# Fourteen small copies moved from VectorE to GpSimd in a scheduled attention kernel, together with a newly searched plan

## Chip, cores and metric

One core of a Trainium2 chip. The metric is the device time of one execution in microseconds (us). An execution's time is about 1.8 us more than the span of its profile, so the two are not mixed below. Every run also reports its span and the mean clock granted to TensorE (1.000 is full speed). All runs told here count as fast.

## The reference

Two attentions on the same x (2048 x 640, bf16), mixed by a gate. Cut:

```python
g = _sigmoid((x * gate_w).sum(-1, keepdims=True))
a = _A_ref(x, A_wqkv, A_wo)   # full softmax attention, 32 heads of 20, 2048 x 2048 scores per head
b = _B_ref(x, B_wqkv, B_wo)   # each token looks at 8 positions, itself first, 2 apart: s, s-2, ..., s-14
return g * a + (1 - g) * b
```

Branch A has 32 x 2048 x 2048 exponentials. They set the time. Branch B is small and is fitted in beside them, 256 tokens at a time.

## The kernel before

The kernel does not write its instruction order down. A list scheduler inside it, run when the program is built, gives each operation an assumed duration and decides what comes next on each engine. The numbers in `PLAN` are its thresholds, changed every few score tiles; they come from an offline search.

```python
PLAN = {
    0: ((0.34, 0.64), 0.37, 6.3, 2.5, 0.51, -1.0, -0.1, 11.8, 4.5, 7.2, 0.52, 0.47, 4.4, 1.86, 0.0, 0.85, 2, 0.0),
    ...                                   # 49 entries in all
}
...
# at score tile s:
plan = PLAN.get(s) if acting else None
if plan:
    (SLACK, XTOL, XPRIO, XLATE, DWAIT, DIDLE, DIDLE2, DTIME, DLOW, DLATE, DVE_AHEAD, DAHEAD, BOOST, XBOOST, RFILL,
     FILL, HOLD, BOFF) = plan
```

The loop over score tiles: TensorE makes 2 or 3 blocks of 128 x 512 scores (`qk`), ScalarE takes their exponentials in one instruction (`exp`), TensorE multiplies the results with V two tiles later (`pv`). Some blocks "ride" along to VectorE, which makes their exponentials by integer arithmetic (`uD`, then shifted copies `eD`). Between tiles the scheduler spends TensorE's free time on projections and on branch B, and where its load is under `FILL`, on filler matmuls with a zero or throw-away result:

```python
def exp(s):
    n = len(tiles[s])
    exps[s] = T("act", actc(512 * n), lambda e: e.activation(
        ebuf[s % NE][:, 0:512 * n], score[s % 2][:, 0:512 * n], ACTF.Exp, scale=LN2 / STEP), ...)

def filler(limit):
    if sch.load(2.3) >= FILL:
        return False
    ...   # four matmuls of 512 columns, each on a quarter of the columns of the array
```

The part touched: each step of branch B needs the last 16 K and V columns of the step before it, and copies them to the front of its tile before the new columns are written.

```python
def TB(dur, *a, **k):          # VectorE work of branch B; bdone paces it against BALL
    bdone[0] += dur
    return T("dve", dur, *a, **k)

if u > 0 and m > 0 and f0 == 0:
    bb, key = ((kB, "kB"), (vB, "vB"))[m - 1]
    TB(0.15, lambda e, bb=bb: e.tensor_copy(bb[:, :, 0:PADB], bb[:, :, TOK:TOK + PADB]),
       reads=[key], writes=[key], port=True)
```

## Time and profile before

| | kernel before |
|---|---|
| time | 836.07 us (835.97 to 836.23, 3 runs) |
| ScalarE busy | 803.9 of 835.4 us |
| ScalarE waiting for scores, after the first exponential | 7.6 us |
| head / middle / tail | 19.6 / 804.2 / 11.6 us |

The head ends at the start of the first exponential, the middle at the end of the last. To read such a kernel, ask of each of the three what sets it: a fixed chain in the head, ScalarE's work and gaps in the middle, TensorE's queue in the tail. The prediction shows the lines.

### The profile page before, as it was taken

What the parts mean: (1) busy time and instruction counts of PE and PEld (TensorE: products, weight loads), DVE (VectorE), ACT (ScalarE), POOL (GpSimd) and SP (SyncE); (2) the same over time, 40 slices, a digit from 0 to 9 for tenths busy, and PEclk for the clock granted to TensorE, in tenths of its full rate; (3) what the DMA queues carried; (4) which work ended last, traced back from release to release, by engine and by line L of the source; (5) the groups of instructions that cost most, each with busy time, mean ns of one, the idle gap of its engine ahead of it and who ended that gap; (6) DMA issues with size and microseconds to landing.
All of it is one profiled execution on the core that took longest, in us unless ns stands there. A gap on an engine that the chain in (4) does not pass through costs nothing.

```text
span 835.4 us, 29602 instructions
## 1 busy us (share of the span) xinstructions
PE 789.3 (94%) x12599; PEld 289.9 (35%) x12601; DVE 683.7 (82%) x1205; ACT 803.9 (96%) x767; POOL 138.7 (17%) x180
## 2 busy tenths in 40 slices
PE   8999999999999899989998999999999999998997
PEld 4333323334333332333233333333333333333223
DVE  7567888889888887978797988798898898887873
ACT  4999999999999999999999999999999999999994
POOL 5013013431111111011111011111102111101110
PEclk9999999999999999999999999999999999999999
DMA  9112112200111110011001011110011001101100
GB/s 313 30 37 44 33 25 45 73 13 19 29 37 29 29 30 20 7 42 32 20 18 41 18 20 29 36 42 9 5 39 30 10 20 25 38 6 31 32 6 34
DMA packets 45016, 29.15 MB, mean 35 GB/s; under 512 B 27204, under 2 KB 43684, under 8 KB 44884
## 3 DMA queue, kind: packets, MB, share of 16 engines
q1 hardware_dynamic: 44596, 26.92, 12.4%
q8 instruction: 100, 1.64, 0.8%
q10 hardware_dynamic: 288, 0.33, 0.1%
q14 instruction: 32, 0.26, 0.1%
HBM read 11.94 MB, written 2.62 MB: 17 GB/s over the span
## 4 chain that ended last, share of the span: by engine, by line
PE 54%; ACT 30%; issue 10%; DVE 5%; DVEq 0%; ACTq 0%
ACT ebuf L1538 30%; PE score L1515 17%; PE obank L1583 13%; PE side L557 13%; PE score L557 5%; PE obank L1604 2%; DVE uD L1528 1%; PE side L1604 1%; DVE eD L797 1%; PE obank L459 1%; PE score L1230 1%; PE side L885 1%; DVE stage L869 0%; PE score L1604 0%; DVE stage L970 0%
## 5 line engine op out<-in xcount | busy, mean ns | idle before, releaser
L1538 ACT ACTIVATE ebuf<-score 128x1024 bf16<-128x1024 f32 (+1 forms) x735 | 792.6, 1237 | 11.6 <-PE score L1515 9.7
L1515 PE MATMUL score<-qT,kT 32*128 32x512 bf16 x2048 | 291.9, 384 | 31.6 <-ACT ebuf L1538 20.6
L1528 DVE TENSOR_SCALAR uD<-score 128x512 int16<-128x512 f32 x324 | 217.2, 683 | 38.4 <-PE score L1515 36.1
L797 DVE TENSOR_SCALAR eD<-uD 128x2048 int16<-128x2048 int16 x243 | 168.1, 722 | 7.9 <-PE obank L1583 7.2
L1515 PEld LDWEIGHTS score<-qT,kT 32*128 32x128 bf16 x2048 | 75.1, 91 | 282.7 <-ACT ebuf L1538 137.6
L1583 PE MATMUL obank<-ebuf,vA 128*21 128x512 bf16 x1724 | 161.3, 385 | 2.2 <-ACT ebuf L1538 1.8
L789 POOL TENSOR_TENSOR vS<-vA,vw 128x252 bf16<-128x252 bf16 x81 | 61.0, 757 | 291.5 <-PE obank L1583 256.3
L557 PE MATMUL side<-xT,kvw 128*32 128x256 bf16 (+1 forms) x2530 | 103.0, 281 | 3.1 <-DVE qkvB L853 1.4
L1583 PE MATMUL obank<-eD,vS 128*21 128x512 bf16 x972 | 84.1, 382 | 0.0
L557 PEld LDWEIGHTS side<-xT,kvw 128*32 128x32 bf16 x2530 | 59.3, 96 | 37.9 <-issue 22.0
L764 POOL TENSOR_TENSOR rcp<-rcp,gA 128x16 f32<-128x16 f32 x31 | 11.3, 365 | 351.9 <-DVE rcp L762 351.9
L1583 PEld LDWEIGHTS obank<-ebuf,vA 128*21 128x21 bf16 x1724 | 38.6, 89 | 82.3 <-issue 69.5
L970 DVE TENSOR_TENSOR stage<-qkvB,repB 128x1280 bf16<-128x1280 bf16 x64 | 52.9, 856 | 0.7 <-DMA repB<-eB 0.7
L869 DVE TENSOR_TENSOR stage<-qkvB 128x1280 bf16<-128x1280 bf16 x64 | 51.4, 830 | 0.1
L853 DVE CAST qkvB<-side 128x512 bf16<-128x512 f32 (+1 forms) x72 | 41.9, 591 | 10.5 <-PE side L557 10.5
L557 PE MATMUL side<-stage,ident 128*32 128x512 bf16 (+1 forms) x736 | 47.4, 345 | 1.2 <-DVE uD L744 0.5
L1604 PE MATMUL obank<-xT,zero 128*32 128x512 bf16 x444 | 37.9, 385 | 0.0
L770 POOL TENSOR_TENSOR oN<-oTt,rcp 128x512 bf16<-128x512 f32 x31 | 33.0, 1065 | 2.4
L1583 PE MATMUL obank<-uD,vA 128*21 128x512 bf16 x324 | 31.7, 382 | 0.0
L758 DVE STREAM_TRANSPOSE oTt<-obank 128x512 f32<-128x512 f32 x32 | 22.7, 709 | 9.0 <-PE obank L1583 8.9
L1583 PEld LDWEIGHTS obank<-eD,vS 128*21 128x21 bf16 x972 | 24.0, 92 | 17.4 <-issue 4.1
L557 PE MATMUL side<-woA_d,oTd 128*32 128x128 bf16 (+1 forms) x580 | 28.8, 293 | 0.0
(173 smaller groups left out, 555.5 us busy)
## 6 DMA issues: line engine op xcount, KB each, us to landing
repB<-eB SPq DMA_DIRECT2D x128, 32.0 KB
WqP<-in_A_wqkv_dram SPq DMA_DIRECT2D x16, 160.0 KB
stage<-in_B_wqkv_dram SPq DMA_DIRECT2D x1, 2400.0 KB
oTd<-oN SPq DMA_DIRECT2D x108, 20.0 KB
qT<-dst SPq DMA_DIRECT2D x104, 20.0 KB
out_dram<-outsb SPq DMA_DIRECT2D x12, 160.0 KB
kvw<-in_A_wqkv_dram SPq DMA_DIRECT2D x2, 800.0 KB
oTd<-in_A_x_dram SPq DMA_DIRECT2D x2, 640.0 KB
```

The source lines that it names most:

```text
L557: ins = e.matmul(o[j:k, :], l(j) if callable(l) else l[:, j:k], r, start=(first and i == 0), stop=(last and i == n - 1), skip_group_check= ...
L770: T(en, c2, lambda e: e.tensor_tensor(oo, ii, ib, ALU.mult), reads=["rcp", "oTt"], writes=["oN0"])
L789: T("pool", 0.7, lambda e: e.tensor_tensor(vS[:, d % 2, :, :], _ap(vA, (kb * NQ + q) * 4 * DV, [[0, K - 1], [1, 4 * DV]]), _ap(vw, 0, [[1, ...
L797: T("dve", 0.11 + 0.1334 * n, lambda e, k=k, sl=sl: e.tensor_scalar(eD[:, sl % NS, 0:512 * n].bitcast(I16), uD[d % 2][:, 0:512 * n].bitcas ...
L853: t = TB(dvc(n * TOK), lambda e, o=o, i=i: e.tensor_copy(o, i), reads=[("side", b)], writes=[key])
L869: TB(dvc(CN * TOK, 2), lambda e, w=w, ks=ks: e.tensor_tensor(prodB(w), qB[:, :, :], ks, ALU.mult), reads=["qB", "kB"], writes=[("prod", w) ...
L970: TB(dvc(CN * TOK, 2), lambda e, w=w, vs=vs, rr=rr: e.tensor_tensor(prodB(w), vs, rr, ALU.mult), reads=["vB", ("repB", w4 % NR)], writes=[ ...
L1515: ins = e.matmul(o, kT[32 * j:32 * j + 32, q, kb * P:(kb + 1) * P], qT[g % NQT][32 * j:32 * j + 32, :], start=True, stop=True)
L1528: t = T("dve", 0.69, lambda e: e.tensor_scalar(uD[d % 2][:, 512 * i:512 * (i + 1)].bitcast(I16), side[x], UOFF, 0.0, op0=ALU.add, op1=ALU. ...
L1538: exps[s] = T("act", actc(512 * n), lambda e: e.activation(ebuf[s % NE][:, 0:512 * n], score[s % 2][:, 0:512 * n], ACTF.Exp, scale=LN2 / S ...
L1583: ins = e.matmul(obank[32 * j:32 * j + DV, :], v, src, start=(kb == 0), stop=(last and k >= len(lst) - 4), skip_group_check=True)
L1604: ins = e.matmul(o[32 * j:32 * j + 32, :], w[:, 32 * j:32 * j + 32] if best else w[:, :], xT[:, 0, 0:512], start=bool(best), stop=bool(bes ...
```

## The change

Intent: take the 14 copies off VectorE, which carries part of the exponentials, put them on GpSimd, which is mostly idle, and search the plan again for that program. The diff, with the plan cut:

```diff
 PLAN = {
-    0: ((0.34, 0.64), 0.37, 6.3, 2.5, 0.51, -1.0, -0.1, 11.8, 4.5, 7.2, 0.52, 0.47, 4.4, 1.86, 0.0, 0.85, 2, 0.0),
-    ...                                             (49 entries)
+    0: ((0.3, 0.64), 0.31, 2.5, 2.5, 0.49, -1.34, -0.1, 11.8, 7.0, 8.15, 0.52, 0.47, 4.4, 4.0, 0.0, 0.71, 2, 0.0),
+    ...                                             (58 entries)
 }
-                TB(0.15, lambda e, bb=bb: e.tensor_copy(bb[:, :, 0:PADB], bb[:, :, TOK:TOK + PADB]), reads=[key], writes=[key], port=True)
+                T("pool", 0.3, lambda e, bb=bb: e.tensor_copy(bb[:, :, 0:PADB], bb[:, :, TOK:TOK + PADB]), reads=[key], writes=[key])
-    BALL = 172.0
+    BALL = 170.0
```

## The prediction

> **What bounds the kernel now.** I began with the page's busy times and its costliest groups.
>
> ```profile
> PE 789.3 (94%) x12599; PEld 289.9 (35%) x12601; DVE 683.7 (82%) x1205; ACT 803.9 (96%) x767; POOL 138.7 (17%) x180
> ...
> L1538 ACT ACTIVATE ebuf<-score 128x1024 bf16<-128x1024 f32 (+1 forms) x735 | 792.6, 1237 | 11.6 <-PE score L1515 9.7
> L1528 DVE TENSOR_SCALAR uD<-score 128x512 int16<-128x512 f32 x324 | 217.2, 683 | 38.4 <-PE score L1515 36.1
> L797 DVE TENSOR_SCALAR eD<-uD 128x2048 int16<-128x2048 int16 x243 | 168.1, 722 | 7.9 <-PE obank L1583 7.2
> ```
>
> ScalarE (ACT) is busy 96% of the span, almost wholly with the exponentials of attention A (L1538). VectorE takes a share of them: 324 blocks of 512 columns (L1528), each later used through shifted copies (L797). The 11.6 us ahead of the L1538 group is everything ScalarE lost there, 9.7 of it waiting for scores. To place it I cut the execution at the first exponential's start and the last one's end; the columns are the stretch, its length, busy time and instruction count of each engine, then TensorE clock and DMA.
>
> ```profile
> 0.00:19.60 19.60, 16.51 (x129) 9.41 (x135) 14.44 (x34) 8.11 (x10) 12.25 (x21) 1.00 0.95 307
> 19.60:823.80 804.20, 765.29 (x12302) 277.04 (x12302) 664.39 (x1162) 794.65 (x755) 126.45 (x159) 1.00 0.11 28
> 823.80:835.40 11.60, 7.48 (x172) 3.47 (x172) 4.90 (x9) 1.10 (x3) 0.00 (x0) 0.98 0.16 59
> ```
>
> So there are a head of 19.6 us, 804.2 us in which ScalarE (fourth engine) is busy 794.65, and a tail of 11.6 us. 2.1 of the 9.7 us waited for scores is the wait before the very first exponential and belongs to the head; **only 7.6 us of ScalarE waiting is left for a better order to win.** ScalarE's own timeline, read for the rows with an idle time in brackets, shows where:
>
> ```profile
> 22.04 3.28 ACT L1538 ACTIVATE ebuf<-score 128x1024 bf16<-128x1024 f32 x3 [0.97 <-PE score L1515]
> 25.64 29.82 ACT L1538 ACTIVATE ebuf<-score 128x1024 bf16<-128x1024 f32 x30 [0.33 <-PE score L1515]
> 56.38 2.37 ACT L1538 ACTIVATE ebuf<-score 128x1536 bf16<-128x1536 f32 x2 [0.92 <-PE score L1515]
> 305.77 61.65 ACT L1538 ACTIVATE ebuf<-score 128x1024 bf16<-128x1024 f32 x59 [0.41 <-PE score L1515]
> 452.67 5.12 ACT L1538 ACTIVATE ebuf<-score 128x1024 bf16<-128x1024 f32 x5 [0.46 <-PE score L1515]
> 458.42 1.45 ACT L1538 ACTIVATE ebuf<-score 128x1536 bf16<-128x1536 f32 x1 [0.64 <-PE score L1515]
> 460.25 11.34 ACT L1538 ACTIVATE ebuf<-score 128x1536 bf16<-128x1536 f32 x9 [0.37 <-PE score L1515]
> ```
>
> They are a few short waits, in groups. The group at 452 to 460 us coincides with the only stretch where the TensorE clock fell (third figure from the end):
>
> ```profile
> 454.60:458.00 3.40, 2.73 (x25) 0.73 0.18 47
> 458.00:461.40 3.40, 3.33 (x57) 0.77 0.04 7
> ```
>
> Last, the tail, from the timeline:
>
> ```profile
> 823.22 0.60 ACT L1538 ACTIVATE ebuf<-score 128x512 bf16<-128x512 f32 x1 [0.18 <-PE score L1515]
> 823.87 0.40 PE L1583 MATMUL obank<-ebuf,vA 128*21 128x512 bf16 x4 [0.30 <-ACT ebuf L1538]
> 826.42 0.45 DVE L772 STREAM_TRANSPOSE oN<-oN 128x256 f32<-128x256 f32 x1
> 830.07 1.27 PE L1063 MATMUL score<-outsb,oN 128*32 128x128 bf16 x32
> ```
>
> The last product with V starts at 823.87; its normalized result is there at 826.87, but the closing projection (L1063) starts only at 830.07, behind 80 projection matmuls of 512 columns that fill TensorE from 825.31. The tail is TensorE's queue, not the chain through VectorE.
>
> **What the Trainium skill says.** "Perfetto Trace Analysis", Identifying the Most-Contended Engine, takes occupancy as the measure for Vector, Scalar and GpSimd and warns that matmul busy time is not one for TensorE. The trace agrees: TensorE shows 94% while ScalarE gets gapless stretches of dozens of exponentials. "TensorE: Matmul & The Clock Gate", Part 1, says that an idle window of about 3.4 us throttles the array's clock; here 0.73 and 0.77 are granted in the two stretches above, after gaps of 0.4 to 0.5 us around 450 to 456 us, and 1.00 in nearly all the rest. "SBUF — State Buffer", Who interferes with whom, says that GpSimd and a VectorE copy in a two-port mode, or one with two SBUF inputs, exclude each other for a whole instruction. GpSimd's L789 takes 610 ns in the median and 1191 at most, which fits, though no row names the cause. "GPSIMD Engine Reference", Engine selection, calls GpSimd about line rate on one-input work; this case has no small one-input copy there yet.
>
> **Part 1, the copies.** The history copies are these (shown before the bar: 14 instructions, 173 ns each):
>
> ```profile
> L840 DVE COPY qkvB<-qkvB 128x80 bf16<-128x80 bf16 x14 | 2.4, 173 | 0.1
> ```
>
> VectorE loses 14 x 0.173 = 2.4 us of 683.7. GpSimd gains 14 copies; from its rcp product (16 columns, 222 ns median) and vS product (252 columns, 610 ns) I estimate 222 + 64 x 388/236 = 0.33 us each, 4.6 us in all on an engine 17% busy. VectorE has 804.2 - 664.4 = 140 us idle in the middle and hands nothing saved straight to ScalarE: in the built program both kernels give VectorE 324 blocks and 243 shifted copies. Direct worth: 0 to 0.3 us; I write 0.
>
> **Part 2, the plan.** The plan only sets thresholds of the scheduler that runs at build time, so I compared the two built instruction orders. Engines do the same work but for these counts:
> - Exponentials: 479 of 1024, 255 of 1536 and one of 512 columns become 469, 262 and none: 735 to 731 instructions, 1724 blocks in both. In gapless stretches of the timeline a fit gives 0.94 us from start to start for 1024 and 1.34 to 1.36 for 1536. 10 x 0.94 + 0.5 - 7 x 1.35 = 0.45; **-0.4 us**.
> - Filler matmuls, which only keep TensorE busy: 748 fall to 536, 53 sets of four. A set adds 0.22 us (four take 0.39 us, eight 0.61), so 11.7 us leave TensorE. They were put where TensorE had time: not on the path.
> - The end. Before, the last exponential (512 columns) is followed by 4 V products, then 16 + 20 + 20 narrow and 80 wide projection matmuls. After, the last one has 1024 columns, and after it stand 8 V products, 4 narrow and the 80 wide ones. From the last exponential's end at 823.82 to 830.07 TensorE needed 6.25 us; now 8 V products (0.43), 4 narrow (0.1) and the wide ones (4.76) make about 5.3, less some 0.25 because the narrow ones moved ahead make the last V products start late: **-0.7 us**.
> - Waits of ScalarE. I weighed the TensorE work between two score groups (columns at the 0.22 us per four above) against the exponentials beside it. Pairs of score tiles whose TensorE work reaches 0.99 of ScalarE's time stand in the kernel before at about 20, 22, 52, 56, 62, 165, 193, 273, 275, 302, 468, 545, 753 us, and waits follow most of them (0.97 and 0.33 at 22, 0.92 at 56, 0.41 at 306). In the new order such pairs are at about 47 (two, the worst at 1.36), 51, 63, 202, 352 (two), 630, 729 us: 9 for 13. Single tiles over 1.1 fall from 57 to 29. Waits of this kind, some 3.2 us before, I put at 2.6.
> - The clock. The four-tile stretch with the least TensorE work before is 0.42 of ScalarE's time, exactly at 452 us. After, the least is 0.42 as well (about 751 us), with 0.44 and 0.45 at 162, 194 and 524. So one dip seems as likely as before: 1.5 us (0.46 + 0.64 + 0.37), put at 1.2.
> - The rest, 7.6 - 3.2 - 1.5 = 2.9 us, follows VectorE's queue (at 710 us three shifted copies ahead of a block) and short late scores. With 2.4 us less on VectorE and a search that looked for such waits, I put it at 2.2.
> Waits: 2.6 + 1.2 + 2.2 = 6.0 for 7.6; **-1.6 us**.
>
> Sum: 836.07 - 0.4 - 0.7 - 1.6 = **833.4 us**.
>
> **Rivals.** (a) GpSimd's queue holds the copy back, and with it VectorE. GpSimd works in order, and its vS products wait for TensorE up to 12.6 us (256.3 us in 44 waits), its rcp products for VectorE up to 23.1. A history copy queued behind one would hold the projection's eviction (L853) that writes the same tile, and in VectorE's order all behind it. For it: in the new order a vS product or a normalization stands right ahead of most of the 14 copies. Against it: VectorE has slack, and the scheduler places the copy in time order. If half the copies cost VectorE 1 us and a third of that reached ScalarE, +2.3 us: 835.7. (b) Fewer fillers let the clock fall in several stretches. At 1.5 us each, three more make 838. Against it: the four-tile stretches below 0.5 of ScalarE's time fall from 16 to 12. (c) The search found nearly all waits: 7.6 to 2 us gives 829.4. Against it: the kernel before came from a search of the same kind, and the plan is chosen by a model that knows neither the clock nor the small spread of real waits. (d) No gain, because chosen and real order differ: only the counts stay, 835.
>
> **Range and chances.** Even with every wait gone and the counted gains the time is 836.07 - 7.6 - 1.1 = 827.4, or 1.0% faster; so over 2% faster (819.3) is out of reach unless something that I don't see shrinks the head. Over 2% slower (852.8) would take ten dips of the clock. (c) and (b) set the range: 830.2 to 836.8.
>
> **What would show it.** ScalarE's L1538 group with 731 instructions and about 792.2 us busy; its wait for scores near 8 (6 and the head's 2.1) instead of 9.7. The stretch from the last exponential's end to the end near 10.9 us instead of 11.6, with L1063 starting 5.4 to 5.6 us after it. The copies on GpSimd at about 0.3 us, and no waits of VectorE's L853 for them beyond 1 us in total. Clock below 1.00 in at most two stretches of 3.4 us. The prediction is wrong if the waits stay at 9.7 or rise, if VectorE shows waits for the copies, or if the tail is no shorter.

## The result, and the profile after

833.12 us median (831.77 to 834.58, 4 runs) against 836.15 us (835.97 to 837.18, 4 runs). A ratio is the mean time of one kernel's fast runs over that of the other's fast runs of the same rounds, so not quite the ratio of these medians: 0.9962, 95% interval 0.9938 to 0.9985. That is faster, but within 2%. The profiled execution (831.99 us) has a span of 830.2 us against 835.4. The page after, in the lines that answer to those of the prediction:

```profile
PE 776.4 (94%) x12389; PEld 284.4 (34%) x12389; DVE 679.5 (82%) x1191; ACT 802.8 (97%) x763; POOL 139.1 (17%) x194
...
L1547 ACT ACTIVATE ebuf<-score 128x1024 bf16<-128x1024 f32 (+1 forms) x731 | 791.4, 1232 | 8.8 <-PE score L1524 6.7
L1537 DVE TENSOR_SCALAR uD<-score 128x512 int16<-128x512 f32 x324 | 217.1, 684 | 41.6 <-PE score L1524 38.9
L806 DVE TENSOR_SCALAR eD<-uD 128x2048 int16<-128x2048 int16 x243 | 169.0, 725 | 5.8 <-PE obank L1592 5.2
```

The exponentials are four fewer and 1.2 us less busy; the wait for scores fell from 9.7 to 6.7 us (24 waits to 11), of which 2.2 us is again the wait ahead of the first. VectorE's share is the same, 324 and 243. The three stretches, cut as before (TensorE, weight loads, VectorE, ScalarE, GpSimd, clock, DMA):

```profile
0.00:19.09 19.09, 16.69 (x131) 9.39 (x135) 13.73 (x35) 8.12 (x11) 12.29 (x21) 1.00 0.95 301
19.09:819.31 800.22, 752.94 (x12138) 272.35 (x12132) 660.86 (x1148) 793.63 (x751) 126.81 (x173) 1.00 0.12 28
819.31:830.20 10.89, 6.76 (x128) 2.71 (x124) 4.90 (x9) 1.08 (x2) 0.00 (x0) 0.91 0.18 62
```

Head -0.5, middle -4.0, tail -0.7 us: together the 5.2 us. In the middle ScalarE is 1.0 us less busy and 3.0 us less idle. Its timeline, four of the rows with a wait after the first exponential (the others are of 0.16 to 0.26 us):

```profile
21.53 24.30 ACT L1547 ACTIVATE ebuf<-score 128x1024 bf16<-128x1024 f32 x25 [0.99 <-PE score L1524]
50.45 7.01 ACT L1547 ACTIVATE ebuf<-score 128x1024 bf16<-128x1024 f32 x6 [1.58 <-PE score L1524]
67.38 3.28 ACT L1547 ACTIVATE ebuf<-score 128x1536 bf16<-128x1536 f32 x3 [0.28 <-PE score L1524]
629.51 1.45 ACT L1547 ACTIVATE ebuf<-score 128x1536 bf16<-128x1536 f32 x1 [0.45 <-PE score L1524]
```

One wait of 1.58 us at 50 us is now a third of all that is left after the first exponential. No stretch of 3.4 us in this execution has a clock under 1.00 between the head and the tail, where the profile before had two (one fall, which lies across both). The 0.91 of the tail is a fall at 828.27 us, after TensorE's last matmul, and costs nothing. In the tail the last V products start at 819.36 and the closing projection at 824.83:

```profile
819.36 0.61 PE L1592 MATMUL obank<-ebuf,vA 128*21 128x512 bf16 x8
824.83 1.27 PE L1072 MATMUL score<-outsb,oN 128*32 128x128 bf16 x32
```

That is 5.52 us after the last exponential's end at 819.31; before it was 6.25. And the copies, first their row of the groups:

```profile
L849 POOL COPY qkvB<-qkvB 128x80 bf16<-128x80 bf16 x14 | 4.4, 313 | 36.7 <-DVE stage L979 36.7
```

then the same kernel's table of waits (us in total, times, longest):

```profile
POOL qkvB L849 <- DVE stage L979: 36.7, 5, 11.6
```

They take 249 ns in the median (245 to 708) in place of 173 on VectorE, wait up to 11.6 us for the last reader of the old columns, and the profile names nobody that waited for them.

### The profile page after: what moved, and what is told of

It is laid out like the page before. It is cut to its first block, busy times and chain, and to the rows that moved or that the text cites. A ratio compares the mean times of both kernels' runs of the same rounds, so it can differ in the third digit from the quotient of the medians.

```text
span 830.2 us, 29189 instructions
## 1 busy us (share of the span) xinstructions
PE 776.4 (94%) x12389; PEld 284.4 (34%) x12389; DVE 679.5 (82%) x1191; ACT 802.8 (97%) x763; POOL 139.1 (17%) x194
## 4 chain that ended last, share of the span: by engine, by line
ACT 49%; PE 34%; issue 13%; DVE 4%; DVEq 0%; ACTq 0%
ACT ebuf L1547 49%; PE score L1524 10%; PE obank L1592 8%; PE side L566 8%; PE score L566 4%; DVE uD L1537 1%; DVE eD L806 1%; PE obank L468 1%; PE score L1239 1%; PE obank L1613 1%; ACT eB L923 0%; PE side L1262 0%; PE score L1613 0%; ACT tB L957 0%; PE score L693 0%
## 5 line engine op out<-in xcount | busy, mean ns | idle before, releaser
L1547 ACT ACTIVATE ebuf<-score 128x1024 bf16<-128x1024 f32 (+1 forms) x731 | 791.4, 1232 | 8.8 <-PE score L1524 6.7
L773 POOL TENSOR_TENSOR rcp<-rcp,gA 128x16 f32<-128x16 f32 x31 | 8.7, 282 | 280.2 <-DVE rcp L771 280.2
L1613 PE MATMUL obank<-xT,zero 128*32 128x512 bf16 x296 | 26.6, 384 | 0.0
L566 PE MATMUL side<-woA_d,oTd 128*32 128x512 bf16 (+2 forms) x520 | 26.0, 295 | 0.0
```

Of the source, the lines that this page charges most:

```text
L566: ins = e.matmul(o[j:k, :], l(j) if callable(l) else l[:, j:k], r, start=(first and i == 0), stop=(last and i == n - 1), skip_group_check= ...
L1547: exps[s] = T("act", actc(512 * n), lambda e: e.activation(ebuf[s % NE][:, 0:512 * n], score[s % 2][:, 0:512 * n], ACTF.Exp, scale=LN2 / S ...
L1613: ins = e.matmul(o[32 * j:32 * j + 32, :], w[:, 32 * j:32 * j + 32] if best else w[:, :], xT[:, 0, 0:512], start=bool(best), stop=bool(bes ...
```

## Experiments

Twelve runs, each beside the kernel before on the same chip. Seven keep one kernel's built order and change one thing in it, and `old_tail` changes only its end. A set is four filler matmuls. Moving a copy to another engine's list while the scheduler still reckons with the old engine leaves the sequence on TensorE, ScalarE and the DMA queue identical, instruction by instruction (I compared the built orders; for ScalarE and VectorE the traces show the same); the plain source edits of `copies_alone` and `plan_alone` do not, and that is their point.

My theory: the order carries all the gain, by shorter waits and a shorter tail; the copies carry none. Rivals: the copies are what gains; or GpSimd's queue costs something that the plan makes good; or the gain is only where TensorE's clock falls.

### new_again and new_again2: the changed kernel, unaltered

> The changed kernel unaltered. Its four times so far fall in two groups, 831.8 and 832.0 (granted clock 1.000 and 0.999) and 834.2 and 834.6 (0.998 twice). Theory: the upper group has one stretch of about 7 us at three quarters of TensorE's clock, as the kernel before has at 456 us in its profile; then again two groups about 2.5 us apart, each time with the clock on its side, and the kernel before near 836.1 in every run with 0.998. Rival: the spread has nothing to do with the clock; then times and clock do not go together. Ratio to the kernel before 0.995 to 0.998.

> The changed kernel once more, as the yardstick of this call. From ten runs so far: 831.8 to 832.0 with the clock at 0.999 or 1.000, 832.8 to 834.6 with 0.997 or 0.998. Theory (falls of the clock and a head that is 0.7 us longer in some runs are all the spread there is): every run with a clock of 0.999 or more within 831.6 to 832.8, every one of 0.998 or less between 832.6 and 835.5; ratio to the kernel before 0.994 to 0.997.

Measured: ratios 0.9942 (0.9928 to 0.9957) and 0.9955 (0.9941 to 0.9969). The profile of `new_again` fell on an execution with a fall of the clock. Two stretches of TensorE (length, busy, clock, DMA), cut where the clock changed:

```profile
512.51:515.92 3.41, 2.07 (x30) 1.00 0.11 29
515.92:519.34 3.42, 3.42 (x45) 0.50 0.40 132
```

and from the timeline of the same execution, TensorE just before and ScalarE just after:

```profile
514.55 0.38 PE L920 MATMUL side<-repB,negRep 32*128 32x512 bf16 x1 [1.28 <-DVE repB L916]
...
518.67 2.04 ACT L1547 ACTIVATE ebuf<-score 128x1024 bf16<-128x1024 f32 x2 [0.83 <-PE score L1524]
```

TensorE stood 1.28 us for VectorE, the clock fell to half for 3.41 us, and ScalarE had a wait of 0.83 us that the profile without the fall does not have. The place lies some 10 us before the one that the count of TensorE work in the prediction named as weak (524 us).

Why one execution has this fall and another not can be read from the kept traces. Their clock record goes in steps of 3.41 us, and where these steps lie against the kernel differs from execution to execution. I added up TensorE's work in each step, counted as in the prediction at 0.22 us per four matmuls of 512 columns (so the shares are estimates). Between the first and the last exponential of all 14 traces the clock falls 16 times, each time after a step that is filled to 0.20 to 0.39; of the 3250 other steps at full clock the emptiest holds 0.376, and only two hold less than 0.39. In `new_again` the step before the fall holds 0.38. In `new_again2` the step there lies 1.4 us earlier against the same order and holds 0.43, and the clock stays:

```profile
511.93:515.34 3.41, 2.08 (x33) 1.00 0.08 17
515.34:518.75 3.41, 3.24 (x59) 1.00 0.35 117
```

The busy time is the same in both, 2.07 and 2.08 us, so it is not the measure; the columns are. In these traces the load within one step decides, and a weak stretch counts only if a step happens to fall on it.

The second spread is the head. The first exponential starts at 18.93 us in `new_again` and at 19.79 in `new_again2`; the kernel before shows both too (19.62 in its profile, 18.88 to 19.66 in its variants below). So the 0.5 us of the head in the comparison above cannot be put down to the change. With both spreads named:

| all runs | runs | mean, us | clock 0.999 or 1.000 | their mean | others' mean |
|---|---|---|---|---|---|
| kernel before | 33 | 837.1 | 8 | 835.7 | 837.6 |
| changed kernel (with the first four) | 16 | 832.9 | 10 | 832.3 | 834.0 |

The first four of the kernel before (mean 836.4 us) are not in the table, as their clocks are not all on record.

The best runs, with full clock and short head, are 835.6 and 831.8 us: 3.8 us apart. The means are 4.2 us apart; falls of the clock add 1.4 us to the mean of the kernel before and 0.6 us to that of the changed one. The expectation that clock and time go together held in the main, though the two groups of `new_again` lay 1.0 to 1.4 us apart and not 2.5, the kernel before did not stay near 836.1 us (835.6 to 839.5 at clocks of 0.994 to 1.000), some runs at 0.997 stay close to 833 (a short head and one fall in the one profiled), and three of the four runs at 0.999 in `new_again2` are over 832.8 (832.5 to 833.1; a long head in the one profiled).

### old_order_pool: the old order with the copies on GpSimd

```diff
-    TB(0.15, ..., reads=[key], writes=[key], port=True)
+    TB(0.15, ..., reads=[key], writes=[key], port=True, eng="pool")   # timed as VectorE's, issued on GpSimd
```

> The order of the kernel before, on every engine the same instructions in the same sequence, with only the 14 history copies taken from VectorE's list and put into GpSimd's at the place where they were scheduled. Theory (the copies are worth nothing by themselves): ratio to the kernel before 0.9995 to 1.0015. Rival 1 (2.4 us less on VectorE reach ScalarE): 0.997. Rival 2 (GpSimd's queue holds copies back, since the order was not made for it): 1.002 or more and VectorE's evictions into the K and V tiles waiting for the copies.

Measured: 838.84 us median, ratio 1.0014 (0.9995 to 1.0033). The ratio includes more falls of the clock (0.994 or 0.995 in four of six runs), which come to the kernel before as well (in three of its eleven). The profile is the cleaner reading. Its middle:

```profile
18.95:822.89 803.94, 764.75 (x12302) 276.76 (x12296) 663.09 (x1148) 794.51 (x755) 130.62 (x173) 1.00 0.12 28
```

and the row of the copies among the groups:

```profile
L842 POOL COPY qkvB<-qkvB 128x80 bf16<-128x80 bf16 x14 | 4.7, 339 | 51.7 <-DVE stage L972 51.7
```

803.94 us against 804.20 of the kernel before, each with one fall of the clock; ScalarE waited 9.7 us for scores in both. The copies stood 51.7 us in GpSimd's queue and nobody waited for them. Worth of the move in this order: 0 to 0.3 us. Both rivals fall. One question stays open: whether the move makes falls of the clock more frequent. Here all six runs are under 0.999, against 9 of 11 of the kernel before; in the new order it is 2 of 6 with the copies on GpSimd (`new_again`) and none of 6 with them on VectorE (next run). Six runs each do not settle it.

### new_order_dve: the new order with the copies on VectorE

```diff
-    T("pool", 0.3, ..., reads=[key], writes=[key])
+    T("pool", 0.3, ..., reads=[key], writes=[key], eng="dve")         # timed as GpSimd's, issued on VectorE
```

> The order of the changed kernel, the same sequence on every engine, with only the 14 copies put back on VectorE where they were scheduled. Theory (the new plan alone carries the gain): the same as the changed kernel of these rounds within 0.5 us, 0.995 to 0.998 of the kernel before. Rival (moving the copies is needed for the gain, or carries part of it): 1 to 2.4 us slower than the changed kernel, ScalarE waiting for scores more than 6.7 us.

Measured: 832.89 us median, ratio 0.9949 (0.9934 to 0.9965); the changed kernel in the same rounds had 831.87. One microsecond slower looks like the rival. The profiles tell it apart: the first and the last exponentials of `new_order_dve`, then of `new_again2`.

```profile
19.66 1.45 ACT L1549 ACTIVATE ebuf<-score 128x1536 bf16<-128x1536 f32 x1 [2.10 <-PE score L1526]
817.83 2.37 ACT L1549 ACTIVATE ebuf<-score 128x1536 bf16<-128x1536 f32 x2 [0.16 <-PE score L1526]
```

```profile
19.79 1.45 ACT L1547 ACTIVATE ebuf<-score 128x1536 bf16<-128x1536 f32 x1 [2.10 <-PE score L1524]
817.97 2.37 ACT L1547 ACTIVATE ebuf<-score 128x1536 bf16<-128x1536 f32 x2 [0.16 <-PE score L1524]
```

From the first start to the last end both take 800.54 and 800.55 us, with the same 6.7 us of waits; the first profile of the changed kernel has 800.22. So the microsecond is, in the profiled run, mostly the long head, which the unaltered kernel shows as well (the other five were not profiled), and the copies are worth 0 to 0.3 us here too.

### copies_alone and plan_alone: each part of the diff by itself, scheduled anew

```diff
 # copies_alone, from the kernel before          # plan_alone, from the changed kernel
-    TB(0.15, ...)                                -    T("pool", 0.3, ...)
+    T("pool", 0.3, ...)                          +    TB(0.15, ...)
-    BALL = 172.0                                 -    BALL = 170.0
+    BALL = 170.0                                 +    BALL = 172.0
```

> The kernel before with the edit of the copies and BALL 170 alone; its old plan then steers a scheduler that now decides otherwise. The built program has 320 blocks on VectorE in place of 324, 504 + 240 exponentials in place of 479 + 255 + 1, and 892 fillers in place of 748. Theory (a plan fits only the program it was searched for): slower, 4 blocks at 0.46 us plus 9 exponentials at about 0.1 us make 2.7 us without any wait, and waits come on top: 839 to 845 us, ratio 1.003 to 1.010. Rival (the copies are a gain in themselves): below 835.

> The changed kernel with the copies back on VectorE in the source and BALL 172, so that the scheduler decides anew with the new plan. The built program has 308 blocks on VectorE in place of 324 and 460 + 273 + 1 exponentials. Theory: 16 blocks more on ScalarE at 0.46 us make 7.4 us; 839 to 847 us, ratio to the kernel before 1.004 to 1.013, much slower than the same sequence with the copies merely moved (832.9). Rival (the plan is good by itself): 831 to 835.

Measured: 863.22 us, ratio 1.0324 (1.0299 to 1.0349), and 857.03 us, 1.0246 (1.0223 to 1.0269). The direction was right, the size far off: I had counted work and waits, and not that branch B would not be done. ScalarE's timeline at the end of `copies_alone`:

```profile
816.52 17.86 ACT L1538 ACTIVATE ebuf<-score 128x1024 bf16<-128x1024 f32 x15 [0.72 <-PE score L1515]
855.97 0.60 ACT L1082 ACTIVATE stage<-side 128x512 bf16<-128x512 f32 x1 [21.59 <-PE side L1063]
```

The exponentials end at 834.4, some 3 us later than even the upper end of my expectation leaves room for, and the execution ends only at 861.2: 27 us in which the last step of branch B and its projections run with ScalarE idle. In `plan_alone` 18 us follow the last exponential. A plan fits only the program that it was searched for; 2.1 us less assumed VectorE work (14 x 0.15) send the scheduler elsewhere from there on. So "the copies alone" or "the plan alone" cannot be judged by editing the source.

### old_order_fill and old_fill2: filler sets in the old order's weak stretches

```diff
 def pv(units, slices):                      # V products
+    pad = 4 * PADS.pop(len(tiles), 0) if begun[g] else 0
     def fn(e):
+        for j in range(pad):
+            e.matmul(obank[32 * (j % 4):32 * (j % 4) + 32, :], zero[:, :], xT[:, 0, 0:512], start=False, stop=False, ...)
         for k, (g, kb, j, v, src) in enumerate(lst):
```

`old_order_fill` puts six sets at tiles 392 to 404, `old_fill2` 26 in all stretches where four tiles give TensorE under 0.54 of ScalarE's time.

> The kernel before with sets of four zero matmuls added ahead of the V products of the score tiles 392 to 404, six sets, all else in the same sequence. Theory: the fall of the clock at 454 to 461 us comes from TensorE standing idle there too often, and costs ScalarE the waits of 0.64 and 0.37 us behind it; with it gone the granted clock is 1.000, the waits there are below 0.3 us, and the time is 1.0 to 1.6 us (0.9980 to 0.9988) below the kernel before. Rival: the waits at 452 to 460 us have other causes and the sets only add work: 1.000 to 1.001, waits unchanged.

> The same for the kernel before: 26 sets in its stretches under 0.54. Its runs in the last call had clocks from 0.994 to 1.000 and times from 835.6 (1.000) to 839.5 (0.994 to 0.995). Theory: at least five of six runs at 1.000 or 0.999, within 0.5 us of 835.6, ratio to the kernel before 0.9975 to 0.999; the gain of the plan without clock is then 835.6 - 831.8 = 3.8 us, and the rest of the gain in the mean is the clock. Rival: clocks and times as spread as before, ratio 1.000 or more, as with the six sets of the last call.

Measured, `old_order_fill`: 837.68 us, ratio 1.0017 (0.9997 to 1.0037). The waits of 0.64 and 0.37 us at 458 and 460 are gone and the clock is 1.00 there, but in its profile the clock fell at 283 to 289 us instead, in another weak stretch of the same order:

```profile
284.60:288.00 3.40, 3.21 (x22) 0.50 0.15 39
288.00:291.40 3.40, 3.40 (x67) 0.78 0.20 54
```

So the falls move among weak stretches from execution to execution; `old_order_pool` and `old_tail` had theirs at 285 to 288 too, and none at 456, without any set there. So it is not shown that the sets removed the fall at 456, and mending one place proves nothing. And the wait of 0.46 us at 452, which I had put to the clock, stayed and grew to 0.68, and in the profile before the clock fell only at 456.15 us: it has another cause.

`old_fill2`: 835.85 us, ratio 0.9988 (0.9970 to 1.0006); all six runs at 0.999 or 1.000, 835.2 to 836.4 us, where the kernel before has 8 of 33. The theory held, though three of the six runs are 0.6 to 0.8 us over 835.6 where 0.5 was expected: low TensorE load is what lets the clock fall in the old order, as the count by steps above shows too. Its profile is the clean one to compare with the changed kernel's, as neither has a fall before TensorE's last matmul. Its middle and tail:

```profile
18.88:822.06 803.18, 768.51 (x12406) 278.94 (x12400) 665.12 (x1162) 794.72 (x755) 126.68 (x159) 1.00 0.12 28
822.06:833.70 11.64, 7.48 (x172) 3.47 (x172) 4.90 (x9) 1.09 (x3) 0.00 (x0) 1.00 0.17 60
```

Against the changed kernel: middle 803.18 to 800.22, -3.0 us, of which ScalarE is 1.1 us less busy and 1.9 us less idle; its waits for scores after the first exponential go from 6.4 to 4.5 us, the same 1.9. Tail -0.75. Sum -3.7 us, which agrees with 835.6 to 831.8 of the best runs.

### new_fill and new_morefill: the same in the new order

> The changed kernel with 19 sets of four zero matmuls added ahead of V products in the stretches where its order gives TensorE least work (four score tiles under 0.54 of ScalarE's time), all else in the same sequence. Theory (TensorE's clock falls only in these weak stretches, and a fall costs 1 to 2.5 us): granted clock 1.000 in every run, all times within 0.3 us of 831.8, none above 832.3. Rival (falls come at random): the upper group of 833 to 834.6 appears as often. Rival 2 (the sets delay scores): all times up by 0.5 us or more.

> The changed kernel with about 100 sets of four zero matmuls more, ahead of V products wherever four score tiles give TensorE under 0.64 of ScalarE's time and no neighbouring pair over 0.85. Theory (more filling keeps the clock up in nearly all weak stretches and costs ScalarE little): clock 0.999 or 1.000 in at least five of six runs and the mean 0.3 to 1 us under that of the changed kernel. Rival (the weak stretches left, where no set fits, are the ones that matter, as the 19 sets of new_fill suggest): the clock falls as often as without; times 0.3 to 1.5 us over the changed kernel, since the sets delay scores.

Measured, `new_fill` (19 sets): 833.80 us, ratio 0.9965 (0.9945 to 0.9984), clock 0.997 or 0.998 in four of six runs. It failed: the sets did not stop the falls. Its profile fell on a run at 1.000, so where they were is not seen. The trace does show that the 19 sets missed one place: none lies between 374 and 524 us, and the fall of `new_again` came after a step at 512 to 516. That the falls of `new_fill` were there is not shown.

`new_morefill` (103 sets): the clock is 0.999 or 1.000 in all six runs, as hoped, but the time is 838.49 us, ratio 1.0017 (1.0002 to 1.0032), far over both expectations. ScalarE's row:

```profile
L1548 ACT ACTIVATE ebuf<-score 128x1024 bf16<-128x1024 f32 (+1 forms) x731 | 794.9, 1212 | 12.0 <-PE score L1525 9.4
```

Waits for scores rose by 2.7 us, and busy time by 3.5 us with the same 731 instructions and a shorter mean duration (1212 for 1232 ns). The exponentials overlap less: one of 1024 columns lasts 1082 ns in the mean (the kernel before), but where no idle time follows, the next starts 904 ns after it in the median. Beside that spacing the exponentials of `new_morefill` lose 2.0 us more than those of the changed kernel at gaps (67 for 46) and 1.8 us more where they follow each other without a gap, but late. So scores that come just in time take overlap away without a wait in the list. TensorE is thus nearer to being the bound than 94% busy or the list of waits tell.

### new_nofill: the new order without fillers

```diff
-    for j in range(4):
-        ins = e.matmul(o[32 * j:32 * j + 32, :], ..., xT[:, 0, 0:512], ...)
+    for j in range(1):
+        ins = e.matmul(o[32 * j:32 * j + 32, 0:8], ..., xT[:, 0, 0:8], ...)
```

> The changed kernel with every filler set cut to one matmul of 8 columns, all else in the same sequence: 536 filler matmuls of 512 columns go. Theory (fillers hold the clock, and what the clock costs is several us): granted clock below 0.985, and each lost 1% of 830 us, that is 8.3 us of half speed per 0.5%, costs ScalarE 3 us or more: above 837. Rival (the fillers do nothing, their removal frees TensorE): clock as before, time 831.8 or less.

Measured: 844.12 us, ratio 1.0075 (1.0048 to 1.0101), clock 0.961 to 0.978. Nine falls between the first and the last exponential, of which this is the first; ScalarE waited 18.1 us for scores in place of 6.7.

```profile
165.60:169.00 3.40, 3.15 (x23) 0.51 0.07 18
169.00:172.40 3.40, 3.40 (x50) 0.50 0.02 6
```

The fillers earn their place: without them the mean is 843.7 us in place of 833.5. The 53 sets fewer that the new order has did no such harm.

### old_tail: the old order with the last two tiles cut 2 + 2

```diff
-        n = 3 if free else 2
+        n = 3 if free and s != 733 else 2
```

> The kernel before, but its last two score tiles have two blocks each in place of three and one, so that its last exponential has 1024 columns and 734 become 735 less nothing else; all before that in the same sequence. Theory (0.7 us of the gain lie in the tail): from the last exponential's end to the end of the span 10.9 us in place of 11.6, and the last exponential ends no later than 0.1 us after that of the kernel before; 0.5 to 0.8 us off the runs at a clock of 1.000 (834.8 to 835.1 in place of 835.6). Rival (the saved piece comes back as a later last exponential): tail shorter, time the same.

Measured: 836.66 us, ratio 1.0002 (0.9982 to 1.0023). The theory fell: the tail became longer, not shorter. From the timeline, the last exponential, the last V products, the closing projection:

```profile
821.95 1.02 ACT L1538 ACTIVATE ebuf<-score 128x1024 bf16<-128x1024 f32 x1 [0.34 <-PE score L1515]
823.02 0.40 PE L1583 MATMUL obank<-ebuf,vA 128*21 128x512 bf16 x4 [1.01 <-ACT ebuf L1538]
829.56 1.27 PE L1063 MATMUL score<-outsb,oN 128*32 128x128 bf16 x32
```

The last exponential ends at 822.97 and the projection starts 6.59 us later (6.25 before, 5.52 in the new order). TensorE stands 1.01 us for the exponential and has 80 narrow and 80 wide matmuls behind it. What shortens the tail is how much projection is done before the last exponential ends, not the shape of the last tile; the new order had 4 narrow ones left after the V products in place of 56.

## Why the prediction was right

833.4 us against 833.12 us. That the two agree within 0.3 us is in part luck, as the last paragraph of this section shows; the steps can now be checked one by one.

- **Copies, "I write 0".** Right. Both transplants put the worth at 0 to 0.3 us. The size of one, 0.33 us estimated, was 0.25 in the median and 0.31 in the mean.
- **Exponentials, -0.4.** Mis-sized. ScalarE is 1.0 to 1.1 us less busy in the middle, and the exponentials 1.2 us. The traces say why. Back to back, exponentials start 0.904 us (1024 columns) and 1.330 us (1536) apart in the median, where the prediction's fit had 0.94 and 1.35; at that spacing the new counts save only 0.2 us. The other 1.1 us come from gaps: an exponential followed by idle time loses its overlap with the next, about 0.17 us, and there are 46 such gaps for 54. The step that failed is the price of a wait: it costs its own length and the lost overlap, and the prediction had only the length.
- **The end, -0.7.** Right: 5.52 us from the last exponential's end to the closing projection, in the stated 5.4 to 5.6; the tail 10.9. `old_tail` shows that the count of projection matmuls left was the reason and not the larger last exponential. Two errors cancelled within it: the last V products did not start 0.25 us late but 0.05 us after the exponential's end, while they and the narrow matmuls took 0.71 us and not 0.53.
- **Waits of the heavy pairs, 3.2 to 2.6; the rest, 2.9 to 2.2.** From 6.1 us in my count (6.4 measured without a fall) 4.8 were foreseen, 4.5 measured; near in sum. Not each in place: the pair at 47 us did give 1.58 us and that at 630 us 0.45, but at 22 us there was no gain (0.97 to 0.99), and at 352 and 729 us no wait came.
- **The clock, "one dip seems as likely as before", -0.3.** Wrong. Falls came in 6 of 16 runs against 25 of 33 and cost the mean 0.6 against 1.4 us. The new order's fall that a profile caught came some 10 us before a stretch that I had named (524 us), and the number of weak stretches did not tell how often the clock falls: the load within one step of 3.41 us does, and where the steps lie differs from execution to execution. In the old order three of the four falls seen in profiles came at 283 to 285 us, at a stretch that I had not named. And the 0.73 and 0.77 that I read at 456 us were one fall to half the clock, of 3.41 us, across both stretches. The wait of 0.46 us, counted with the clock, did not belong to it.
- **Rivals.** (a) The copies did stand in GpSimd's queue, up to 11.6 us, for the last reader of the old columns and not for vS products, and nobody waited. (b) Fewer fillers did not let the clock fall more often; without any it did, in every run. (c) and (d) lie on either side of what came.

Without the clock's luck the change is worth 3.8 us (0.45%), where the sum without its clock term was 2.4 us; ScalarE's busy time (-1.1 for -0.4) and the waits (-1.9 for -1.3) are the terms that were too small. It came out at 3.0 us: the median of the four runs of the kernel before lay 0.5 us over its best (836.15 for 835.6), that of the changed kernel 1.3 us over (833.12 for 831.8), as two of its four had a fall. So a sum that was 1.4 us short met a record that the clock and the head had made 0.8 us smaller than the gain.

No version tried beats the changed kernel: `old_fill2` removes the falls from the old order and stays 3 us behind, and filling the new order failed twice.

## What to carry to other kernels

When a scheduler decides the order, split the change by moving instructions inside the built order, not by editing the source: here each half of the diff alone looked 2 to 3% bad, and one half is in truth worth nothing. Cut the execution at the first start and the last end of the bounding engine, and compare the three parts in executions with the same clock; a tenth of a per cent is read there when medians cannot give it. Work off the path was worth nothing to move here; the order of work in front of the bounding engine was worth all of it.

## What the Trainium skill lacked or had wrong

- "TensorE: Matmul & The Clock Gate", Part 1, gives an idle window of about 3.4 us as what throttles the clock. Here it fell without a window that was idle throughout: the longest standstill that the profile shows just ahead of the fall of `new_again` was 1.28 us, with matmuls on either side. Another passage of Part 1, "A second HAM failure mode: psum-queue depth-cycling", does tell of falls from short idle times between matmuls. What the page lacks is the load below which to expect one: by the estimate above, about 0.38 of a step of 3.41 us (16 falls after 0.20 to 0.39, 3250 other steps at 0.376 or more).
- "ScalarE: Activation LUTs", Rules for kernel authors, budgets about 0.3 us per instruction plus 0.83 ns per element for a bias that is read through a pointer (an estimate of 1.15 us for 1024 columns), which is too much here. Its section "What ACT_TABLE_LOAD costs" has figures that come near: 186 ns plus 0.833 ns per element without such a bias (an estimate of 1.04 us), and an overlap of about 93 ns between instructions back to back. Here one of 1024 columns takes 1.02 us after idle time and the next starts 0.90 us after it, an overlap of 0.12 us. What the page lacks is that a gap costs the overlap on top of its own length, about 0.17 us each here (7.9 us in 46 gaps).
- "GPSIMD Engine Reference", Engine selection, says that one-input work is roughly at line rate. A copy of 128 x 80 bf16 took 249 ns in the median and up to 708 on GpSimd, 173 ns on VectorE. The page has no figure for such small copies.
